# Turning the state's weights on the vector engine in 16 pieces, and a new place for the normalisation, in a fused attention and gated feed-forward kernel

## The chip, the cores and the metric

The kernel runs on one core of a Trainium2 chip. The metric is the device time of one execution in microseconds (us). Runs of a kernel before and of a changed kernel were taken in turn on the same chip.

## The reference, cut to what matters

```python
# x: (8, 8, 512, 64), state: (8, 8, 32, 64)
a      = softmax(scale * x @ state.T);   xread = a @ state     # per batch and head
a2     = softmax(scale * state @ x.T);   sread = a2 @ x
tokens = concat(xread, sread)            # per batch 512 + 32 rows of 512 columns
h      = tokens @ w_in                   # 512 -> 2048
out    = (h * cos(h)) @ w_out            # 2048 -> 512
```

`a` is the side of the tokens, `a2` that of the state. `a2` is computed with the state's rows on the partitions and the 512 tokens along them. For `a2 @ x` it has to stand the other way round, with the tokens on the partitions. This turning is what the change is about.

## The kernel before

Each batch of 512 tokens is worked through in 16 steps, one tile of 128 hidden columns each. The batch's own attention is prepared in the steps of the batch before it, in the gaps. A step's work, by engine:

- PE: `hidden` (L469 in the profile of before), the two products that make a tile of h; then `output`, the products of the tile of three steps ago with w_out (L534).
- ACT and DVE in turn, the gates: `gate` (ACT, L475), `gate2` (DVE, L478), `gate3` (ACT Abs and Sin, L483 and L484), `gate4` (DVE, L490). `gate4` frees the PSUM tile of h, of which there are two, so `hidden` of step s+2 waits for `gate4` of step s.
- In the gaps: PE makes `products` 0 to 3 (the four quarters of state @ w_in, from which `hidden` is made) and `reads` 0 and 1 (the two halves of `a2 @ x`). ACT does `exps`, the exponentials of both softmaxes. DVE does `spread1`, which lays maxima and sums out along the rows, and `norm1`.

The outputs use sums and differences of blocks (seven products for eight). Batches go in pairs, and the accumulators are two pairs of PSUM banks, MAIN and SIDE. At the end of phases 0 and 2, that is in step 10 of each batch, MAIN is copied out, one half by ACT and one by DVE:

```python
def keep_product(out, bank):
    nc.scalar.activation(out.t[:, 0], acc[bank][0], func=ACTF.Copy, scale=TWO_PI)
    nc.vector.tensor_scalar(out.t[:, 1], acc[bank][1], TWO_PI, None, op0=ALU.mult)
```

The turning and what follows it (note that `a2T` takes the place of `spread`):

```python
self.spread, self.z2 = xT[:, 0:2], xT[:, 2:4]          # z2: exp on the state's side
self.a2T = xT[:, 0:2].rearrange("p j (c m) -> p j c m", c=NC)
def turn(self, j):                       # PE, 4 transposes of 128x128 into PSUM
    for c in range(NC):
        nc.tensor.transpose(out=at[j][:, P * c:P * c + P],
                            in_=self.z2[:, j, P * c:P * c + P], identity=ident)
def turn_kept(self, j):                  # ACT, copy from PSUM
    nc.scalar.copy(self.a2T[:, j].rearrange("p c m -> p (c m)"), at[j])
def norm1(self):                         # DVE, a = exp * (1 / sum)
    nc.vector.tensor_tensor(self.aT, self.z1, self.spread, op=ALU.mult)
```

A plan says in which step each part is issued. The lists `x_dve` and `x_act` are issued between `gate2` and `gate3` of the step, `y_act` and `y_dve` behind `gate4`. `later` holds delayed adds and stores, of which one is issued per step ("the pop"). Each engine works in the order of issue.

```python
gate(t); gate2(t); go(1); go(3)          # go(1): x_act, go(3): x_dve
...
gate3(t)
if later: later.pop(0)()
gate4(t)
...
go(2); go(4)                             # y_act, y_dve
...
output(line.pop(0))                      # step 10: ends with keep_product
```

## Time and profile before

| | before |
|---|---|
| median of the first 3 runs | 792.2 us (791.26 to 793.64) |
| median of the 6 runs beside the changed kernel | 791.51 us (791.21 to 793.64) |
| span of the profiled execution | 789.4 us |
| PE busy | 767.3 us (97%) |
| DVE / ACT busy | 431.2 / 389.3 us |

PE's busy share bounds the time.

### The profile page before, as it was taken

The numbers are of one execution on the slowest core, as the hardware profiler recorded it, in microseconds if no ns is written. First come the engines' busy times: TensorE is split into PE (matmuls) and PEld (weight loads), VectorE is DVE, ScalarE is ACT, GpSimd is POOL, SyncE is SP. The second block draws the span as 40 slices with busy tenths as digits, with TensorE's granted clock in tenths as the row PEclk, the third lists the DMA queues.
The fourth block names the chain that finished last, engine by engine and source line by source line (L and its number), as shares of the span: only waits on it lengthen the run. The fifth ranks groups of instructions, "written<-read, shape, count | busy, mean of one in ns | idle before, by whom it ended". The sixth has DMA issues, their size and how long they took to land.

```text
span 789.4 us, 7555 instructions
## 1 busy us (share of the span) xinstructions
PE 767.3 (97%) x2664; PEld 340.4 (43%) x2664; DVE 431.2 (55%) x675; ACT 389.3 (49%) x626; POOL 178.7 (23%) x119
## 2 busy tenths in 40 slices
PE   8998999899999999999999999999999999999997
PEld 3442333344344344444444434434444444455554
DVE  5879887732564467744554467635553545431531
ACT  3877964644364445643473446443563445322222
POOL 3343359684000000551000000740000004610200
PEclk9999999999999999999999999999999999999999
DMA  8485461051010610150003410340100114000021
GB/s 239 160 248 179 127 140 28 0 90 18 0 27 14 107 27 14 30 104 0 15 14 54 80 27 7 53 75 0 27 1 0 27 27 117 17 0 15 14 41 40
DMA packets 161957, 43.49 MB, mean 55 GB/s; under 512 B 153920, under 2 KB 153920, under 8 KB 161920
## 3 DMA queue, kind: packets, MB, share of 16 engines
q1 hardware_dynamic: 161024, 42.49, 24.7%
q10 hardware_dynamic: 768, 0.39, 0.2%
q8 instruction: 21, 0.34, 0.2%
q0 software_dynamic: 128, 0.13, 0.1%
q14 instruction: 16, 0.13, 0.1%
HBM read 34.08 MB, written 8.91 MB: 54 GB/s over the span
## 4 chain that ended last, share of the span: by engine, by line
PE 80%; ACT 9%; DVE 8%; issue 1%; DMA 1%; POOL 1%; SPq 0%; DVEq 0%; POOLq 0%
PE o L534 44%; PE h L469 26%; PE at L316 4%; PE o L654 3%; PE at L406 2%; DVE q L478 1%; ACT q L483 1%; ACT q L484 1%; DVE g_all L490 1%; ACT s L227 1%; ACT q L475 1%; DVE xT L336 1%; ACT xT L362 1%; DVE aT L383 1%; PE o L316 1%
## 5 line engine op out<-in xcount | busy, mean ns | idle before, releaser
L469 PE MATMUL h<-aT,sw 128*128 128x512 f32 x512 | 243.2, 598 | 10.8 <-DVE g_all L490 10.2
L534 PE MATMUL o<-g_all,w_out 128*128 128x512 f32 x512 | 236.4, 598 | 1.1 <-POOL w_out L241 1.1
L496 POOL TENSOR_TENSOR g_all<-g_all 128x512 f32<-128x512 f32 x80 | 112.1, 1424 | 450.8 <-DVE g_all L490 447.2
L475 ACT ACTIVATE q<-h 128x512 f32<-128x512 f32 (+1 forms) x144 | 82.2, 571 | 261.7 <-PE h L469 261.6
L478 DVE SCALAR_TENSOR_TENSOR q<-q,h 128x512 f32<-128x512 f32 (+1 forms) x144 | 94.2, 654 | 207.3 <-ACT q L475 207.3
L534 PE MATMUL o<-g_all,s 128*128 128x512 f32 x384 | 177.3, 598 | 0.0
L490 DVE TENSOR_TENSOR g_all<-h,q 128x512 f32<-128x512 f32 (+1 forms) x144 | 94.8, 658 | 123.9 <-ACT q L484 117.7
L469 PEld LDWEIGHTS h<-aT,sw 128*128 128x128 f32 x512 | 96.8, 191 | 136.2 <-issue 110.2
L534 PEld LDWEIGHTS o<-g_all,w_out 128*128 128x128 f32 x512 | 94.0, 190 | 125.5 <-issue 118.4
L483 ACT ACTIVATE q<-q 128x512 f32<-128x512 f32 (+1 forms) x144 | 87.6, 608 | 96.3 <-DVE q L478 96.3
L534 PEld LDWEIGHTS o<-g_all,s 128*128 128x128 f32 x384 | 70.9, 190 | 91.7 <-issue 87.3
L484 ACT ACTIVATE q<-q,halfpi 128x512 f32<-128x512 f32 (+1 forms) x144 | 100.5, 698 | 4.5
L241 POOL TENSOR_TENSOR w_out<-w_out,s 128x1024 int32<-128x1024 int32 x10 | 23.9, 2389 | 79.4 <-DVE w_out L236 79.4
L496 DVE TENSOR_TENSOR g_all<-g_all 128x512 f32<-128x512 f32 x48 | 33.2, 692 | 1.6
L443 ACT COPY sw<-at 128x512 f32<-128x512 f32 x50 | 26.8, 589 | 9.0 <-PE at L316 9.0
L469 PE MATMUL h<-sT,w_in 128*128 128x256 f32 x128 | 30.2, 379 | 0.0
L654 PE MATMUL o<-w_out,g_all 128*128 128x512 f32 x64 | 29.6, 592 | 0.0
L469 PEld LDWEIGHTS h<-sT,w_in 128*128 128x128 f32 x128 | 24.3, 190 | 10.1 <-issue 6.2
L316 PE MATMUL at<-w_in,stT 64*32 64x512 f32 x400 | 27.2, 601 | 0.0
L241 POOL TENSOR_TENSOR w_in<-w_in,s 128x1024 int32<-128x1024 int32 (+1 forms) x10 | 19.7, 1966 | 32.1 <-DVE w_in L236 18.6
L540 DVE SCALAR_TENSOR_TENSOR held<-o,held 128x512 f32<-128x512 f32 x40 | 25.3, 676 | 2.3 <-PE o L534 2.3
L561 DVE STREAM_TRANSPOSE ot<-held 128x512 f32<-128x512 f32 x32 | 22.2, 692 | 0.0
(83 smaller groups left out, 443.5 us busy)
## 6 DMA issues: line engine op xcount, KB each, us to landing
out_dram<-ot SPq DMA_DIRECT2D x132, 64.0 KB, 2.0
g_all<-in_moe_w_out_dram SPq DMA_DIRECT2D x8, 1024.0 KB, 4.9
g_all<-in_moe_w_in_dram SPq DMA_DIRECT2D x6, 1024.0 KB, 5.2
xT<-in_x_dram SPq DMA_DIRECT2D x96, 64.0 KB, 2.3
x_b<-in_x_dram SPq DMA_DIRECT2D x24, 256.0 KB, 4.7
x_b<-in_x_dram SPq DMA_DIRECT2D x16, 128.0 KB, 3.9
g_all<-in_moe_w_in_dram SPq DMA_DIRECT2D x4, 512.0 KB, 6.0
x_b<-in_moe_w_out_dram SPq DMA_DIRECT2D x1, 1024.0 KB, 6.1
```

The costliest lines, as they stand in the source:

```text
L241: nc.gpsimd.tensor_tensor(bits, bits, e.bitcast(I32), op=ALU.add)
L316: nc.tensor.matmul(out=(to or at)[j][Ns * k:Ns * k + Ns, 0:n], lhsT=w[D * j:D * j + D, self.b, Ns * k:Ns * k + Ns], rhs=r(slice(D * j, D * ...
L443: (copy or nc.scalar.copy)(sw_of[self.b, nt][:, j, c0:c1], to[j][:, 0:c1 - c0])
L469: nc.tensor.matmul(out=t.hp, lhsT=t.lhs(i), rhs=t.rhs(i), start=(i == 0), stop=(i == t.kn - 1))
L475: nc.scalar.activation(t.q, t.hp, func=ACTF.Copy, bias=MAGIC)
L478: nc.vector.scalar_tensor_tensor(out=t.q, in0=t.q, scalar=MAGIC, in1=t.hp, op0=ALU.subtract, op1=ALU.subtract)
L483: nc.scalar.activation(t.q, t.q, func=ACTF.Abs)
L484: nc.scalar.activation(t.q, t.q, func=ACTF.Sin, bias=halfpi, scale=-TWO_PI)
L490: nc.vector.tensor_tensor(t.g, t.hp, t.q, op=ALU.mult)
L496: engine.tensor_tensor(out, a, b, op=ALU.subtract)
L534: nc.tensor.matmul(out=acc[bank][ch], lhsT=w[:, i, P * ch:P * ch + P], rhs=g.g, start=(i == 0), stop=(i == NH - 1))
L654: nc.tensor.matmul(out=acc[MAIN][i], lhsT=t.g[:, P * i:P * i + P], rhs=w_out[:, :, t.f, :], start=(t.n_th == 0), stop=(t.n_th == NF - 1))
```

## The change

The intent: PE no longer turns `a2` for batches 2 to 7. DVE does it, in 16 pieces of 32 partitions. `norm1` of these batches moves behind `gate4`, so that the gate need not wait for it. The pop moves behind `gate4` in steps where `x_dve` has work. Other parts shift by some steps to make room.

```diff
+        def turn_block(self, k, q):
+            src = self.z2.rearrange("p j (c q i) -> p q (j c) i", q=P // 32, i=32)
+            dst = self.a2T.rearrange("p j c m -> p (j c) m")
+            rows = slice(Ns * k, Ns * k + Ns)
+            nc.vector.transpose(out=dst[32 * q:32 * q + 32, :, rows],
+                                in_=src[rows, q])
 ...
-            x_dve[s[6]].append((b, "norm1"))
+            (x_dve if b == 1 else y_dve)[s[6]].append((b, "norm1"))
 ...
-            pairs(s[0], b, "turn", "turn_kept", 0)
+            if b < 2:
+                pairs(s[0], b, "turn", "turn_kept", 0)
 ...
+        def blocks_turned(b, to):
+            for i in range(16):
+                to[i * 5 // 16].append((b, "turn_block", i % NK, i // NK))
 ...
-                prod(14, b + 1, 0)
-                early(b + 1, (1 + (b == 1), 2 + (b == 1), 5, 6, 7, 8, 9))
-                late(b + 1, (10, 11, 12, 15))
+            if b + 1 < B and odd:
+                prod(13, b + 1, 0)
+                early(b + 1, (2, 3, 5, 6, 7, 8, 9))
+                blocks_turned(b + 1, (x_dve[12], y_dve[12], x_dve[13],
+                                      y_dve[13], x_dve[14]))
+                pe[15].append((b + 1, "reads", 0))      # reads 1: next step 0
+            elif b + 1 < B:
+                early(b + 1, (4, 5, 6, 7, 8, 9, 10))
+                blocks_turned(b + 1, (y_dve[10], x_dve[11], y_dve[11],
+                                      x_dve[12], y_dve[12]))
+                late(b + 1, (None, 13, 14))
+                prod(15, b + 1, 0)
 ...
-        if later:
+        if later and not todo[3]:                       # todo[3]: x_dve
             later.pop(0)()
         gate4(t)
 ...
+        if later and todo[3]:
+            later.pop(0)()
         go(4)
```

Left out: batch 1's products 3 are copied by ACT instead of DVE, five conversions of weights come a step later, six of the GpSimd blocks come one step later and two ten, the turning of the tokens comes one or three steps later, other products move by one or two, and in step 3 the copy of batch 0's products 1 moves behind `gate3`.

More of the change, by code (lines that the diff above doesn't have):

```diff
@@ L395, in turn_kept @@
                            at[j])
+        def turn_block(self, k, q):
+            src = self.z2.rearrange("p j (c q i) -> p q (j c) i", q=P // 32,
+                                    i=32)
+            dst = self.a2T.rearrange("p j c m -> p (j c) m")
+            rows = slice(Ns * k, Ns * k + Ns)
+            nc.vector.transpose(out=dst[32 * q:32 * q + 32, :, rows],
+                                in_=src[rows, q])
         def reads(self, j):
@@ L752, in prod @@
             pe[s].append((b, "products", nt) + bank)
-            if b == 1 and nt > 0:
+            if b == 1 and 0 < nt < 3:
                 x_dve[s].append((b, "products_taken", nt) + bank)
@@ L768, in early @@
                 for k in range(NK):
-                    to = (x_dve, y_dve)[k % 2]
+                    to = (x_dve, y_dve)[k % 2 * (k < 2)]
                     to[s[k // 2]].append((b, "tokens_turned", k))
@@ L778, in early @@
             y_dve[s[5]].append((b, "spread1"))
-            x_dve[s[6]].append((b, "norm1"))
+            (x_dve if b == 1 else y_dve)[s[6]].append((b, "norm1"))
         def late(b, s):
-            pairs(s[0], b, "turn", "turn_kept", 0)
-            pe[s[1]].append((b, "reads", 0))
+            if b < 2:
+                pairs(s[0], b, "turn", "turn_kept", 0)
+            if s[1] is not None:
+                pe[s[1]].append((b, "reads", 0))
             pe[s[2]].append((b, "reads", 1))
@@ L804, in plan @@
         else:
+            odd = b % 2
             bank = (SIDE,) if b == 1 else ()
@@ L807, in plan @@
                 turned(1, 0)
-            prod(0, b, 1, *[MAIN for _ in bank])
-            prod(4, b, 2, *bank)
-            prod(9, b, 3, *bank)
-            if b + 1 < B:
-                prod(14, b + 1, 0)
-                early(b + 1, (1 + (b == 1), 2 + (b == 1), 5, 6, 7, 8, 9))
-                late(b + 1, (10, 11, 12, 15))
+                prod(0, b, 1, MAIN)
+            elif odd:
+                prod(0, b, 1)
+                turned(b, 1)
+            else:
+                late(b, (None, None, 0))
+                prod(2, b, 1)
+                turned(b, 3)
+            prod(4, b, 2, *bank)
+            prod(9 if odd else 10, b, 3, *bank)
+            if b + 1 < B and odd:
[10 more added lines that the diff above has]
+                prod(15, b + 1, 0)
         return pe, x_act, y_act, x_dve, y_dve
     conv_at = {s: 4 + i for i, s in enumerate(
-        (0, 1, 2, 3, 4, 5, 6, 7, 8, 10, 11, 12, 13, 14))}
+        (0, 1, 2, 3, 4, 5, 6, 7, 8, 11, 12, 13, 14, 15))}
     conv_at.update({B * NF + 5: N_LOADS, B * NF + 7: N_LOADS + 1})
@@ L825 @@
     lo, hi = slice(0, NH // 2), slice(NH // 2, NH)
-    block_at = {15: (ALU.add, s1, a21, a22, lo),
-                17: (ALU.add, s1, a21, a22, hi),
-                18: (ALU.subtract, s2, s1, a11, lo),
-                19: (ALU.subtract, s2, s1, a11, hi),
-                20: (ALU.subtract, s4, a12, s2, lo),
-                21: (ALU.subtract, s4, a12, s2, hi),
-                22: (ALU.subtract, s3, a11, a21, lo),
-                23: (ALU.subtract, s3, a11, a21, hi)}
+    block_at = {16: (ALU.add, s1, a21, a22, lo),
+                18: (ALU.add, s1, a21, a22, hi),
+                19: (ALU.subtract, s2, s1, a11, lo),
+                20: (ALU.subtract, s2, s1, a11, hi),
+                21: (ALU.subtract, s4, a12, s2, lo),
+                22: (ALU.subtract, s4, a12, s2, hi),
+                32: (ALU.subtract, s3, a11, a21, lo),
+                33: (ALU.subtract, s3, a11, a21, hi)}
     LAG = 3
@@ L871 @@
                 part(0, "products", 1, SIDE)
-                part(0, "products_kept", 1, SIDE)
             go(1)
@@ L881 @@
         gate3(t)
-        if later:
+        if step == 3:
+            part(0, "products_kept", 1, SIDE)
+        if later and not todo[3]:
             later.pop(0)()
```

## The prediction

> **What bounds the kernel now.** I read the page's busy row, then the waits sorted by length, then PE alone in 10 us stretches, and last the timeline of one odd and one even batch.
>
> ```profile
> PE 767.3 (97%) x2664; PEld 340.4 (43%) x2664; DVE 431.2 (55%) x675; ACT 389.3 (49%) x626; POOL 178.7 (23%) x119
> PE 80%; ACT 9%; DVE 8%; issue 1%; DMA 1%; POOL 1%; SPq 0%; DVEq 0%; POOLq 0%
> ...
> PE h L469 <- DVE g_all L490: 10.2, 9, 2.7
> ```
>
> The first line is the share of busy time, the second the chain that ended last, the third the only PE wait of any size: `hidden` waits for `gate4` (L490) to give back one of its two PSUM tiles. PE has work in 767.3 of 789.4 us. Of the 22 idle us, 3.2 lie in the first 10 us and 5.0 in the last 10, where nothing changes. From 160 to 780 us the stretches show PE at 10.00 of 10 us, except 320:330 and 490:500 (9.29 each), in the middle of batches 3 and 5. So nearly any PE time taken away comes off the end, and any wait put before PE is added to it. DVE, at 55%, has room on average, but it works in program order, and the gates of each tile stand in that same queue.
>
> **What the turning costs PE.** Batch 4, in order of time (start, duration, engine, line):
>
> ```profile
> 409.36 1.21 DVE L383 TENSOR_TENSOR aT<-aT,xT 128x1024 f32<-128x1024 f32 x1
> ...
> 409.62 1.88 PE L469 MATMUL h<-aT,sw 128*128 128x512 f32 x4
> ...
> 411.33 1.04 PE L389 MATMUL at<-ident,xT 128*128 128x128 f32 x8
> ...
> 412.20 3.60 PE L534 MATMUL o<-g_all,w_out 128*128 128x512 f32 x8
> ```
>
> From 411.33 to 412.20 the eight transposes hold PE for 0.87 us. There is no penalty around them: `hidden` before takes 409.62 to 411.33 = 1.71 us, and the next starts at 415.64, after 3.44 us for eight matmuls, both the ordinary pace (429 ns each).
>
> **What the Trainium skill says.**
> - "VectorE: DVE Perf Modes", section "The three transpose paths": the vector engine transposes only 32x32 blocks, TensorE a full 128x128 into PSUM. Hence 16 pieces, which together move the blocks; and the copy from PSUM (L394) goes. The trace agrees in that L394 exists only for PE's way: 16 copies of 576 ns.
> - "TensorE: Matmul & The Clock Gate", section "Part 4: PE-mode transpose": about 275 ns in a kernel. L389's mean is 273 ns, but that is latency; eight take 0.87 us, 109 ns each, and that is what is saved.
> - "VectorE: DVE Perf Modes", section "Two Vector instructions with no wait between them": an instruction starts only when all before it are done, if its start quadrant differs from theirs. The pieces change their input quadrant each time. `keep` does so today, and the trace agrees: four of 285 ns take 1.18 us, a step of 298 ns, while two same-quadrant subtractions (L353) of 680 ns take 1.28 us, a step of 600.
> - "Advanced Engine Details and Errata", section "The Read-Write Bubble": a fixed latency per instruction, so small pieces pay it each. The next lines agree.
>
> ```profile
> L561 DVE STREAM_TRANSPOSE ot<-held 128x512 f32<-128x512 f32 x32 | 22.2, 692 | 0.0
> L336 DVE STREAM_TRANSPOSE xT<-i 128x1024 f32<-128x1024 f32 x16 | 19.8, 1236 | 0.0
> ...
> L416 DVE TENSOR_TENSOR sr<-at,i 32x128 f32<-32x128 f32 x32 | 9.1, 285 | 0.3
> ```
>
> 512 elements take 692 ns and 1024 take 1236: 1.06 ns each and about 150 fixed. A piece has 32 partitions by 8 blocks by 32 = 256 elements: estimate 420 ns, with a step of about 435.
>
> **The change, part by part.**
> 1. *Removed:* 6 batches x 8 transposes, 6 x 0.87 = 5.2 us of PE, on the path; 12 copies x 576 ns = 6.9 us of ACT, beside PE.
> 2. *Added:* 96 pieces x 435 ns = 42 us of DVE (431 becomes about 473), 7.0 us per batch. Between gate2 and gate4 DVE waits some 1.45 us for ACT's Abs and Sin (timeline of a step: gate2 ends 3.2 us after the start of `hidden`, gate4 starts at 4.75). Three pieces (1.3 us) fit; four (1.74) push gate4 by 0.3.
> 3. *Moved:* `norm1` from between gate2 and gate4 to behind gate4; the pop of the delayed adds and stores behind gate4 where the slot is taken; reads, products, conversions and four GpSimd blocks by one to ten steps, their number unchanged. Each `products` or `reads` costs PE 1.02 us plus two switches of 0.1 wherever it stands.
>
> *Odd batches 3 and 5 (turning for 4 and 6).* The exps, with a table load before and after them, make the gates of steps 8 to 10 late:
>
> ```profile
> 323.43 0.65 DVE L478 SCALAR_TENSOR_TENSOR q<-q,h 128x512 f32<-128x512 f32 x1
> ...
> 324.00 1.80 DVE L383 TENSOR_TENSOR aT<-aT,xT 128x1024 f32<-128x1024 f32 x1
> ...
> 325.73 0.70 DVE L561 STREAM_TRANSPOSE ot<-held 128x512 f32<-128x512 f32 x1
> ...
> 326.36 0.65 DVE L490 TENSOR_TENSOR g_all<-h,q 128x512 f32<-128x512 f32 x1
> ...
> 327.06 1.98 PE L469 MATMUL h<-aT,sw 128*128 128x512 f32 x4 [0.71 <-DVE g_all L490]
> ```
>
> Without the turn PE wants the last of these at 325.3. Now `norm1` no longer stands before gate4(9), but step 8's store transpose moves behind gate4(8), where nothing hides it: gate2(9) comes at 324.1, the second store transpose follows, Abs and Sin end at 326.15, gate4(9) at 326.95. PE waits 1.65 us instead of 0.71. `hidden` of step 12 then starts at 332.15; before, at 333.53, with 1.2 us of reads that now stand elsewhere. Gain 0.2 us a batch. The pieces, in steps 12 to 14, lie beside steps of 5.16 us or more with reads in step 15: no wait.
>
> *Batch 1.* Nothing is delayed there, and the copy of products 3 (1.28) and `norm1` (2.11) both leave the slot of step 9. gate4(9) ends at about 154.25 instead of 155.93; PE, without its turn, wants it at 154.1. `hidden` of step 12 moves from 162.46 (161.26 without the reads) to 159.5: gain 1.75 us, of which 0.87 is the turn.
>
> *Even batches 2, 4, 6 (turning for 3, 5, 7).* Today they have no PE idle. I count from `hidden` of step 8, which now holds the exps. By the trace's same stretch around its own exps (394.67: the late gate4 starts at 407.02) gate4(9) starts at 12.35. Then: spread1 to 14.15; gate2(10); gate4(10) 16.3 to 17.0; norm1 1.2; four pieces 1.74; keep_product 0.69, so gate2(11) only at 20.5; three pieces, gate4(11) to 23.35; three pieces; gate2(12) at 24.65; three pieces; gate4(12) to 27.5; the last three to 28.8. PE reaches reads(0) of step 13 at 3.44 + 5.16 + 6.36 + 5.16 + 5.16 + 1.72 = 27.0. So reads(0) waits about 1.9 us, where 0.87 was saved: a loss of 1.0 us a batch. With pieces of 0.33 us there would be hardly a wait.
>
> *Batch 0.* A conversion leaves step 10 and one is added at step 15; the long waits there (2.67 us at 80.09, 1.78 at 107.28) come from steps 9 and 14, which keep theirs. I put 0.
>
> *Sum:* -1.75 - 2 x 0.2 + 3 x 1.0 = +0.9 us as reckoned. The wait for the pieces is the shakiest term: their duration is extrapolated, and the slots look as if sized so that they just fit. I take 1.0 us for it in place of 1.9, so +0.1 a batch, and get -1.75 - 0.4 + 0.3 = -1.9 us: 790.3 us.
>
> **The rivals.**
> - *All PE time comes off and no wait appears.* For it: PE at 10.00 of 10 us in the even batches, DVE at 4 to 7 of 10. Then 5.2 + 0.9 = 6.1 us: 786. Against it: the DVE queue as added up for steps 9 to 12.
> - *DVE's queue becomes the bound after the exps.* Gate2 of steps 11 and 12 stands behind 7 us of pieces. If a piece takes 0.5 us or more, or is further delayed by the gates, the even batches lose 2 us or more each and the odd ones have gate4(12) late: 795 to 797.
> - *The reload of tokens comes late.* reads(1) now stands in step 0 or 14, and the tokens are turned four steps later instead of five. Against it: in batch 4 sixteen loads are issued within some 14 us and land 2.3 us after (page), and four steps last 20 us or more. If it fails, each batch waits 1 to 2 us, 6 to 10 us in all.
> - *GpSimd's block differences (s3) in steps 32 and 33 come late for step 35.* Two blocks of 2.4 us, POOL idle there: no effect.
>
> **Range and chances.** The three ways reach from 786 to 797; runs of the kernel before spread over 2.4 us. Range 785.5 to 795.0. Two per cent is 15.8 us, three times all that the turn costs PE. Faster by over 2% would need the start-up stretch to shrink by 10 us; slower by over 2% would need two rivals together. Chances: 0.02, 0.96, 0.02.
>
> **What would show it.** L389 with 16 instructions and about 2.1 us instead of 8.3; L394 four copies; a new DVE group of 96 transposes of about 420 ns; DVE busy about 473 us, PE about 762. PE waiting for DVE at `reads` (L406) in three even batches, 0.5 to 2 us each; `hidden` waiting up to 1.7 us in steps 10 and 11 of batches 3 and 5; less of it in batch 1. I am wrong if the pieces differ much from 420 ns, if reads never wait (then 786 or so), or if tokens_turned waits for a DMA.

## The result, and the profile after

The changed kernel took 799.05 us (median of 6 runs, 796.7 to 799.91) against 791.51 us. The ratio was 1.0087, with a 95% interval of 1.0069 to 1.0105. The change made the kernel slower by 0.9%. The time lies outside the range of the prediction, 785.5 to 795.0.

How the lines read: a wait line has the waiting engine, tile and line, what it waited for, the total in us, the number of waits and the longest. A line of a group ends with the number of instructions, busy us, the mean of one in ns, and idle us before them. A line of a timeline has start and duration in us, engine, line, operation, output and inputs, and the number of instructions; a bracket gives the idle time before and what ended it.

First the page's busy row and chain, then PE's waits (total us, times, longest us), then the groups of pieces and of PE's remaining transposes, all of the changed kernel. Line numbers have moved: `hidden` is L479, `output` L544, `gate4` L500, `keep_product` L555 (ACT) and L557 (DVE), the reads L416, the pieces L404.

```profile
PE 767.4 (96%) x2616; PEld 336.4 (42%) x2616; DVE 471.1 (59%) x769; ACT 384.5 (48%) x616; POOL 181.3 (23%) x119
...
PE 69%; DVE 14%; ACT 12%; issue 2%; DMA 1%; POOL 1%; SPq 0%; DVEq 0%; POOLq 0%
```

```profile
PE h L479 <- DVE g_all L500: 11.4, 9, 2.7
PE o L544 <- DVE held L557: 4.3, 5, 1.2
PE o L544 <- ACT held L555: 3.5, 2, 1.7
...
PE at L416 <- DVE xT L404: 0.6, 3, 0.2
```

```profile
L404 DVE STREAM_TRANSPOSE xT<-xT 32x256 f32<-32x256 f32 x96 | 41.8, 436 | 1.9
...
L389 PE MATMUL at<-ident,xT 128*128 128x128 f32 x16 | 2.1, 276 | 0.0
```

The chain that ended last has 69% PE instead of 80%, and DVE and ACT together 26% instead of 17%. The pieces cost what was expected, 436 ns each, and PE has 48 transposes fewer (2616 matmuls instead of 2664). Its busy time did not fall all the same: `hidden` was busy 1.2 us longer in all (244.4 for 243.2), `output` 2.6 (416.3 for 413.7) and the reads 1.3 (18.8 for 17.5). Four matmuls of `hidden` behind a wait show 1.98 us for 1.88, and 3.52 where they ran at half clock (at 105.36; the clock is treated below). What is new are 7.8 us of waits that did not exist before: `output` waits for `keep_product`, 4.3 us for DVE's half and 3.5 us for ACT's.

To see where the time went I compare stretches in which both kernels do the same work: from the start of products 2 of one batch (step 4) to that of the next, read from PE's timeline in the profiled executions.

| stretch, us | before | after |
|---|---|---|
| start to batch 1 | 125.97 | 125.58 |
| batch 1 to 2 | 83.27 | 81.83 |
| batch 2 to 3, 4 to 5, 6 to 7 | 85.05 each | 86.2 each |
| batch 3 to 4 | 86.02 | 90.23 |
| batch 5 to 6 | 86.02 | 88.54 |

Each even batch loses 1.2 us (3 x 1.2 = 3.5), batches 3 and 5 lose 4.2 and 2.5, the first two rows win 1.8. The sum is 8.4 us, which is the difference of the spans (797.7 - 789.4 = 8.3) within the reading.

**An odd batch, before.** The timeline of the kernel before in batch 3, behind the lines that the prediction shows: gate2 and Sin of step 10, ACT's and DVE's half of `keep_product`, and PE's products of step 11.

```profile
327.64 0.68 DVE L478 SCALAR_TENSOR_TENSOR q<-q,h 128x512 f32<-128x512 f32 x1
...
329.02 0.72 ACT L484 ACTIVATE q<-q,halfpi 128x512 f32<-128x512 f32 x1
...
329.99 3.70 PE L534 MATMUL o<-g_all,s 128*128 128x512 f32 x8
330.12 0.60 ACT L545 ACTIVATE held<-o 128x512 f32<-128x512 f32 x1
...
331.11 0.69 DVE L547 TENSOR_SCALAR held<-o 128x512 f32<-128x512 f32 x1
```

Of the eight matmuls the first four go to SIDE and the last four to MAIN. They reach MAIN at 329.99 + 4 x 0.43 = 331.7. ACT had left its half at 330.7, and DVE leaves the other at 331.8, which the last two want at 332.6. Nothing waits, because PE had spent time on the turn and on reads(0) just before.

**An odd batch, after.** The same place in batch 5, which has no half-clock spell (see below):

```profile
502.66 1.98 PE L479 MATMUL h<-aT,sw 128*128 128x512 f32 x4 [1.39 <-DVE g_all L500]
...
503.25 2.29 DVE L383 TENSOR_TENSOR aT<-aT,xT 128x1024 f32<-128x1024 f32 x1
504.48 1.88 PE L544 MATMUL o<-g_all,s 128*128 128x512 f32 x4
505.46 0.67 DVE L488 SCALAR_TENSOR_TENSOR q<-q,h 128x512 f32<-128x512 f32 x1
...
506.83 0.72 ACT L494 ACTIVATE q<-q,halfpi 128x512 f32<-128x512 f32 x1
507.46 0.58 ACT L555 ACTIVATE held<-o 128x512 f32<-128x512 f32 x1
...
508.09 1.13 PE L544 MATMUL o<-g_all,s 128*128 128x512 f32 x2 [1.73 <-ACT held L555]
...
508.92 0.68 DVE L557 TENSOR_SCALAR held<-o 128x512 f32<-128x512 f32 x1
...
509.65 1.13 PE L544 MATMUL o<-g_all,s 128*128 128x512 f32 x2 [0.44 <-DVE held L557]
```

Read it backwards. PE's matmuls into MAIN wait until 508.09 for ACT's copy. That copy is ready to run as soon as PE has ended step 10, but in ACT's queue it stands behind Abs and Sin of step 10. These wait for gate2 of step 10 (505.46), and gate2 stands behind `norm1`, which takes 2.29 us here and 1.22 in the even batches. GpSimd is at work beside it here and idle there. From the times it looks as if one of the two waits for the other: in batch 1 `norm1` took 1.21 us beside GpSimd (at 153.77), and there two GpSimd instructions took 3.53 us, for 2.51 in the same place before. No run takes GpSimd away, so this is not shown. Then DVE's copy stands behind gate4 in the same way, and PE waits again. With the longer wait for `hidden` (1.39 us instead of 0.71) the batch has 3.56 us of waits in place of 0.71.

**An even batch, after.** Batch 2, where there was no wait at all before:

```profile
243.02 0.58 ACT L555 ACTIVATE held<-o 128x512 f32<-128x512 f32 x1
...
243.82 1.22 DVE L383 TENSOR_TENSOR aT<-aT,xT 128x1024 f32<-128x1024 f32 x1
245.07 1.77 DVE L404 STREAM_TRANSPOSE xT<-xT 32x256 f32<-32x256 f32 x4
246.78 0.64 DVE L557 TENSOR_SCALAR held<-o 128x512 f32<-128x512 f32 x1
...
247.48 1.13 PE L544 MATMUL o<-g_all,w_out 128*128 128x512 f32 x2 [1.15 <-DVE held L557]
...
254.60 1.38 DVE L404 STREAM_TRANSPOSE xT<-xT 32x256 f32<-32x256 f32 x3
255.40 0.43 PE L416 MATMUL at<-x_b,xT 128*64 128x128 f32 x2
...
256.03 1.09 PE L416 MATMUL at<-x_b,xT 128*64 128x128 f32 x14 [0.20 <-DVE xT L404]
```

`norm1` and four pieces stand before DVE's half of `keep_product`, and PE waits 1.15 us for it. Later PE starts reads(0) and must stop for the last pieces. The two waits (1.35 us) and the slow restarts behind them, some 0.7 us, are more than the 0.87 us saved.

**The clock.** The ten microseconds from 330 in the changed kernel (columns: PE, PEld, DVE, ACT and POOL busy, then the granted clock, DMA share, GB/s):

```profile
330.00:340.00 10.00, 7.92 (x14) 3.27 (x15) 5.53 (x10) 4.83 (x9) 6.21 (x5) 0.83 0.00 0
```

The single microseconds from 334 to 337 show 0.50, half the clock. A mean of 0.83 over 10 us is then 3.4 us at half clock: 1.7 us of PE's work lost. Such a spell followed the waits of batch 3 but not the same waits of batch 5, which explains 4.2 us there against 2.5. (In the third run below no spell fell into these two batches, and their stretches took 87.96 and 87.94 us.) The profiled execution of before has one spell in the working stretch, at 80 us; that of the changed kernel has two, at 105 and 334.

### The profile page after: what moved, and what is told of

It is laid out like the page before. It is cut to its first block, busy times and chain, and to the rows that moved or that the text cites. A ratio compares the mean times of both kernels' runs of the same rounds, so it can differ in the third digit from the quotient of the medians.

```text
span 797.7 us, 7549 instructions
## 1 busy us (share of the span) xinstructions
PE 767.4 (96%) x2616; PEld 336.4 (42%) x2616; DVE 471.1 (59%) x769; ACT 384.5 (48%) x616; POOL 181.3 (23%) x119
## 4 chain that ended last, share of the span: by engine, by line
PE 69%; DVE 14%; ACT 12%; issue 2%; DMA 1%; POOL 1%; SPq 0%; DVEq 0%; POOLq 0%
PE o L544 37%; PE h L479 22%; PE o L664 3%; PE at L316 3%; DVE q L488 3%; ACT q L493 3%; ACT q L494 3%; DVE g_all L500 2%; DVE xT L404 2%; PE at L416 2%; ACT xT L362 1%; ACT q L485 1%; DVE xT L336 1%; ACT L494 1%; ACT aT L357 1%
## 5 line engine op out<-in xcount | busy, mean ns | idle before, releaser
L479 PE MATMUL h<-aT,sw 128*128 128x512 f32 x512 | 244.4, 600 | 12.4 <-DVE g_all L500 11.4
L544 PE MATMUL o<-g_all,w_out 128*128 128x512 f32 x512 | 237.2, 599 | 4.6 <-DVE held L557 3.5
L506 POOL TENSOR_TENSOR g_all<-g_all 128x512 f32<-128x512 f32 x80 | 114.8, 1456 | 453.4 <-DVE g_all L500 453.3
L544 PE MATMUL o<-g_all,s 128*128 128x512 f32 x384 | 179.1, 600 | 4.4 <-ACT held L555 3.5
L500 DVE TENSOR_TENSOR g_all<-h,q 128x512 f32<-128x512 f32 (+1 forms) x144 | 95.2, 661 | 112.7 <-ACT q L494 109.1
L479 PEld LDWEIGHTS h<-aT,sw 128*128 128x128 f32 x512 | 97.3, 192 | 138.7 <-issue 113.6
L544 PEld LDWEIGHTS o<-g_all,w_out 128*128 128x128 f32 x512 | 93.8, 190 | 130.7 <-issue 120.7
L544 PEld LDWEIGHTS o<-g_all,s 128*128 128x128 f32 x384 | 70.9, 190 | 100.1 <-issue 87.2
L404 DVE STREAM_TRANSPOSE xT<-xT 32x256 f32<-32x256 f32 x96 | 41.8, 436 | 1.9
L479 PE MATMUL h<-sT,w_in 128*128 128x256 f32 x128 | 30.2, 379 | 0.0
L479 PEld LDWEIGHTS h<-sT,w_in 128*128 128x128 f32 x128 | 24.3, 190 | 10.1 <-issue 6.2
```

What stands on the lines that cost most here:

```text
L404: nc.vector.transpose(out=dst[32 * q:32 * q + 32, :, rows], in_=src[rows, q])
L479: nc.tensor.matmul(out=t.hp, lhsT=t.lhs(i), rhs=t.rhs(i), start=(i == 0), stop=(i == t.kn - 1))
L500: nc.vector.tensor_tensor(t.g, t.hp, t.q, op=ALU.mult)
L506: engine.tensor_tensor(out, a, b, op=ALU.subtract)
L544: nc.tensor.matmul(out=acc[bank][ch], lhsT=w[:, i, P * ch:P * ch + P], rhs=g.g, start=(i == 0), stop=(i == NH - 1))
```

## The experiments

Theory A, formed from these traces: the pieces are not dear. Time is lost because work was put before `gate2` and `keep_product` in DVE's queue, and PE waits for the bank MAIN; and in the even batches because reads(0) comes too early for the last pieces. Rival B: the pieces load DVE and slow everything. Rival C: the moved products and reads cost PE the time. All kernels were compared with the kernel before on the same chip. "Even" and "odd" in the results are the stretches of the table above, from batch 2 to 3 and from 5 to 6 (before 85.05 and 86.02, changed kernel 86.22 and 88.54).

### The pieces left out

```diff
-                to[i * 5 // 16].append((b, "turn_block", i % NK, i // NK))
+                pass
```

> The changed kernel without its 96 pieces; the reads take stale weights, so the state rows are wrong on purpose. Theory A (the loss of the even batches is the pieces standing before keep_product and before reads in the vector engine's queue, the loss of the odd batches is norm1 and the popped store standing before gate2 of step 10): even batches lose their waits of 1.15 + 0.2 us and the slow restarts, some 2.0 us each, odd batches stay as they are: 799 - 6 = 793 us, still slower than before (791.5), with the wait of 1.7 us on ACT's keep_product still there in batches 3 and 5. Rival B (the pieces load DVE and slow all): faster than before, 786 or so, and no wait on keep_product left. Rival C (PE's loss comes from the moved products and reads alone): 799, unchanged.

Measured: 793.23 us, ratio 1.0018 (1.0003 to 1.0033), state rows wrong as intended. Even 84.18, odd 88.54. PE's waits:

```profile
PE o L544 <- ACT held L555: 3.5, 2, 1.7
...
PE o L544 <- DVE held L557: 0.9, 2, 0.4
```

The even batches gain exactly what the turn costs (85.05 - 84.18 = 0.87), the odd ones are as slow as with the pieces. So the pieces cost 2.0 us in each even batch, through the waits, and nothing in the odd ones. Even with the pieces free, the changed kernel is not faster than before. Rival B falls, and C for the even batches; for the odd ones the next run and the one with `keep_product` earlier decide.

### norm1 back before gate4

```diff
-            (x_dve if b == 1 else y_dve)[s[6]].append((b, "norm1"))
+            x_dve[s[6]].append((b, "norm1"))
```

> Only norm1 put back before gate4 for all batches. Theory A: in batches 3 and 5 the wait for gate4 grows from 1.40 to about 2.5 us, but the wait on ACT's keep_product (1.73) disappears and that on DVE's stays near 0.4, so 0.5 to 1.5 us gained in each odd batch; in batch 1 some 0.8 us lost; even batches the same or slightly worse: 797 to 799 us. Rival B (pieces): no change, 799. If norm1's place were the whole cause: 791 to 793.

Measured: 791.66 us, ratio 1.0001 (0.9986 to 1.0016). Even 84.94, odd 86.93, batch 1 82.03 (81.83 with the change). PE's waits:

```profile
PE o L544 <- DVE held L557: 0.9, 2, 0.4
...
PE at L416 <- DVE xT L404: 0.6, 3, 0.2
```

My expectation was a miss by 5 us. In the odd batches it held: 1.6 us gained each, no wait on ACT's half. But I had left out that `norm1` stands before `keep_product` in the even batches as well. Taken from there it goes into the time in which DVE waits for ACT anyway, the wait of 1.15 us disappears, and each even batch gains 1.3 us. With 3 x 1.3 + 2 x 1.6 = 7.1 us, putting `norm1` back takes away nearly the whole loss. In the even batches it is not the only cause: without the pieces the loss is gone there as well. `norm1` and the pieces are one queue in front of PE, and what the two runs gain must not be added.

### The pop back before gate4

```diff
-        if later and not todo[3]:
+        if later:
             later.pop(0)()
 ...
-        if later and todo[3]:
-            later.pop(0)()
```

> Only the pop of the delayed adds and stores put back before gate4 in every step. Theory A: in batches 3 and 5 gate2 of step 9 comes 0.65 us earlier, the wait for gate4(9) falls from 1.40 to about 0.75 us and the wait on ACT's keep_product is unchanged at 1.7: about 1.3 us gained in all, 797.5 us. Rival B: no change. If the pop were the whole cause: 793 or less.

Measured: 796.06 us, ratio 1.006 (1.0043 to 1.0076). Even 86.21, odd 87.94. In batches 3 and 5 the wait for `gate4` fell from 1.40 to 0.81 us and that on ACT's half stayed at 1.72. The pop's new place costs 0.6 us in each odd batch and nothing in the even ones. The median fell by more than twice 0.6; the profiled execution had one spell at half clock, the changed kernel's two, and I don't assign the rest.

### Both back

The two diffs above together.

> norm1 and the pop both back. Theory A: the odd batches are about what they were before the change less the turn, some 2 us faster each than in the changed kernel, plus a half-clock spell fewer (1.7 us): 793.5 to 796 us; the even batches keep their 1.15 + 0.2 us of waits. Rival B: no change, 799.

Measured: 790.4 us, ratio 0.9985 (0.9969 to 1.0002). Even 84.95, odd 86.52. It came out better than expected because of the even batches, as in the second run. No wait for ACT's half was left. The turn is gone from PE, and yet nearly nothing is gained: the next runs ask where it went.

### PE's turn taken out of the kernel before, nothing put in

```diff
-            pairs(s[0], b, "turn", "turn_kept", 0)
+            if b < 2:
+                pairs(s[0], b, "turn", "turn_kept", 0)
```

> The kernel before with nothing but PE's 48 transposes and their copies taken out (no pieces, nothing moved; state rows wrong on purpose). If every transpose were on the path: 791.5 - 5.2 = 786.3 us. If, as the trace of before suggests, in batches 1, 3 and 5 the PE only waits longer for gate4(9) (0.98 to 1.85 us, and 0.71 to 1.58 twice), the gain is only that of the three even batches: 3 x 0.87 = 2.6 us, 789 us.

Measured: 789.81 us, ratio 0.9973 (0.9956 to 0.9989), state rows wrong as intended. Even 84.17, odd 86.02, batch 1 83.27. PE's waits for `gate4` in this kernel:

```profile
PE h L469 <- DVE g_all L490: 12.9, 9, 2.7
```

Before it was 10.2 us in as many waits. The difference of 2.7 us is 3 x 0.87: in batches 1, 3 and 5 PE waits for `gate4` of step 9 as much longer as it works less. So of the 5.2 us of transposes only those of the three even batches, 2.6 us, were on the path. (In the start-up a PE wait of 1.7 us for a copy by ACT is new, where the kernel before had its spell at half clock and this execution has none; the stretch to batch 1 took 126.11 us for 125.97.)

### reads(0) of the even batches beside reads(1)

On top of "both back":

```diff
-                late(b + 1, (None, 13, 14))
+                late(b + 1, (None, 14, 14))
```

> norm1 and pop back as in the fourth run, and in the even batches reads(0) moved from step 13 to 14, beside reads(1), which takes away its wait for the last pieces without touching the pieces. If that wait is where the even batches' gain of 0.87 us went: an even batch falls from 84.95 to about 84.0 us, no PE wait on pieces left, 790.4 - 3 x 0.95 = 787.5 us. If the pieces cost something else (a slower DVE or PE beside them): 84.9 again and 790.

Measured: 788.53 us, ratio 0.996 (0.9943 to 0.9976), correct. Even 83.99, odd 86.52. No PE wait on L404 is left. The even batches' gain had gone into the wait for the last pieces, and it comes back with a step more, with the pieces where they were. The total is 1 us above the expectation; the profiled execution had three spells at half clock in the working stretch, at 79, 106 and 151 us.

### keep_product earlier, norm1 where the change put it

```diff
+            if s == 10 and t.b in (1, 3, 5):
+                while len(line) >= LAG:
+                    output(line.pop(0))
             go(1)
             go(3)
 ...
+        if s == 10 and t.b in (2, 4, 6):
+            while len(line) >= LAG:
+                output(line.pop(0))
         go(4)
```

> The changed kernel with norm1 where the change put it, and only keep_product emitted earlier: in the odd batches behind gate2 of step 10, in the even ones before norm1 and the pieces. If the bank held by keep_product is the way by which norm1's new place costs time: odd batches lose their waits of 1.73 and 0.44 us and fall from 88.5 to about 86.1 us; even batches lose the wait of 1.15 us but then wait as much longer at reads(0) for the last pieces (0.2 becomes about 1.8), so stay near 86.2. In all 2 x 2.4 us and a half-clock spell: 792.5 to 794.5 us. If the bank isn't the way: 799.

Measured: 794.74 us, ratio 1.0034 (1.0019 to 1.0049), correct. Even 86.24, odd 86.35. PE's waits:

```profile
PE h L479 <- DVE g_all L500: 11.5, 10, 2.7
PE at L416 <- DVE xT L404: 4.7, 6, 1.1
```

This shows the way. No wait on `keep_product` is left, in any batch; the odd batches fall by 2.2 us although `norm1` stands where it stood. In the even batches the wait moved to reads(0): 1.57 us in each (4.7 / 3), in place of 1.15 and 0.20. The last piece sets the end there, whichever of PE's two waits it is booked under. The total is just above the expected 794.5 us; the profiled execution had a spell at half clock in batch 4, from 430 to 433, and that stretch took 87.94 us.

### norm1 moved in the kernel before

```diff
-            x_dve[s[6]].append((b, "norm1"))
+            (x_dve if b == 1 else y_dve)[s[6]].append((b, "norm1"))
```

> The kernel before with norm1 of batches 2 to 7 moved behind gate4, nothing else. If norm1's new place is harmful by itself: +7 us as between the changed kernel and the second run, 798 us. If it is harmful only once PE's turn and reads no longer stand between the products of steps 10 and 11 (before, PE reaches the bank at 331.7 in batch 3, after ACT has left it at about 331.6), then no PE wait on keep_product appears, an odd batch gains up to 0.7 us and the whole is 790 to 792 us.

Measured: 791.8 us, ratio 1.0012 (0.9995 to 1.0029), correct. Even 85.05, odd 86.92, batch 1 82.02.

```profile
PE h L469 <- DVE g_all L490: 7.8, 6, 2.7
PE at L406 <- ACT xT L394: 3.2, 2, 1.6
```

Neither side of the expectation was right for the odd batches. The wait for `gate4` is gone there, as the change intended, but PE now waits 1.6 us at reads(0) for ACT's copy of the turned weights. The timeline of batch 3 in this run:

```profile
325.58 2.29 DVE L383 TENSOR_TENSOR aT<-aT,xT 128x1024 f32<-128x1024 f32 x1
...
327.94 0.59 ACT L394 COPY xT<-at 128x512 f32<-128x512 f32 x1 [3.25 <-PE h L469]
...
328.58 1.09 PE L406 MATMUL at<-x_b,xT 128*64 128x128 f32 x16 [1.61 <-ACT xT L394]
```

The copy overwrites the tile (`xT`, the part named `spread`) from which `norm1` reads, and it starts when `norm1` has ended, at 325.58 + 2.29 = 327.87. The page books ACT's wait under PE, whose turn had long been done (it started at 322.31 and takes 1.04 us), so I read it by the times. In all the move loses 0.9 us in an odd batch of the kernel before and nothing in an even one; in batch 1 it gains 1.25. By itself it costs little. In the changed kernel it costs the 7 us of the second run: in the odd batches with the turn and reads(0) gone from between the products of steps 10 and 11, in the even ones with the pieces behind it in the queue.

### Only the pieces, on the kernel before

```diff
-            pairs(s[0], b, "turn", "turn_kept", 0)
+            if b < 2:
+                pairs(s[0], b, "turn", "turn_kept", 0)
 ...
-                prod(14, b + 1, 0)
+                prod(13, b + 1, 0)
 ...
-                late(b + 1, (10, 11, 12, 15))
+                to = (x_dve[11], y_dve[11], x_dve[12], y_dve[12], x_dve[13])
+                for i in range(16):
+                    to[i * 5 // 16].append((b + 1, "turn_block", i % NK, i // NK))
+                late(b + 1, (None, 14, 14, 15))
```

`turn_block` is the one of the change.

> The kernel before with only the pieces in place of PE's turn: pieces in steps 11 to 13, both reads in step 14, products 0 of the next batch in step 13; norm1, pops, conversions, tokens and batch 1's products as before. If the pieces cost nothing where no wait hangs on them: even batches 85.05 - 0.87 - 0.2 = 84.0 us, odd batches 86.0 to 86.5 (their gain is eaten by the wait for gate4(9)), in all 788.5 to 790 us. If the pieces slow DVE or PE in themselves: 791 or more.

Measured: 788.0 us, ratio 0.9956 (0.9941 to 0.997), correct. Even 83.82, odd 86.16. The core of the change alone, with the pieces where almost nothing hangs on them (PE waits 0.23 us on DVE's half in batches 3 and 5), is a small gain. The 42 us of DVE work are nearly free: with the turn simply left out (above) the stretches were 84.17 and 86.02. Against that run the even batch also has both reads in one step.

### A version that beats both

On top of "reads(0) beside reads(1)", for the odd batches:

```diff
-                early(b + 1, (2, 3, 5, 6, 7, 8, 9))
+                early(b + 1, (2, 3, 5, 6, 7, 8, 10))    # norm1 in step 10
 ...
+            if s == 10 and t.b in (1, 3, 5):            # keep_product behind gate2
+                while len(line) >= LAG:
+                    output(line.pop(0))
             go(1)
             go(3)
 ...
-        if later:
+        if later and not (t.b in (3, 5) and s in (8, 9, 10)):
             later.pop(0)()
```

> The fifth run, and in the odd batches 1, 3 and 5 norm1 in step 10 between gate2 and gate4, the outputs of step 10 (with both halves of keep_product) right behind gate2, and no pops in steps 8 to 10 of batches 3 and 5. If the odd batches' loss is made of the wait for gate4(9) (1.4 to 1.6 us) and for keep_product alone, both nearly vanish: an odd batch falls from 86.5 to about 85.0 us and the whole to 783.5 to 785.5 us, about 1% faster than before the change. If something else holds them: 787.

Measured: 786.1 us, ratio 0.9924 (0.9905 to 0.9944), correct. Odd 85.25. The even stretch from batch 2 is 84.34, with one wait of 0.25 us on DVE's half; the other two are 83.99 and 83.98. The total is 0.6 us above the expected range. PE's waits for `gate4`, and the one left on `keep_product`:

```profile
PE h L479 <- DVE g_all L500: 9.8, 8, 2.7
...
PE o L544 <- DVE held L557: 0.3, 1, 0.3
```

The wait for `gate4` in batches 3 and 5 is 0.81 us each, where "both back" had 1.58. Three things were moved at once for the odd batches; no run says what each of them gave. The same kernel again, with more rounds:

> The sixth run's kernel again, with more rounds for a narrower interval: 784.5 to 787 us, ratio 0.991 to 0.994.

Measured: 785.68 us (4 runs, 783.74 to 785.71), ratio 0.992 (0.9906 to 0.9935). By the ratio it is 0.8% faster than the kernel before; by the medians, taken on different chips, it is 1.7% faster than the changed one (785.68 / 799.05).

## Why the prediction was wrong

It gave 790.3 us, 1.9 us less than before; measured were 7.5 us more. Its chance of 0.96 for less than 2% either way held (0.9% slower), its range did not. Point by point, by its own steps:

- **The bound and the pieces: right.** The cost of a piece (estimate 420 ns with a step of 435; 436 ns measured, four in 1.77 us) and DVE's sum (estimate 473 us; 471.1) held, and in the odd batches the pieces cost nothing, as it says. PE's busy time did not: some 762 us were expected and 767.4 measured, for the reasons given with the profile after.
- **Batch 1: right in size.** Predicted -1.75 us; the stretch shortened by 1.44, and the start-up, put at 0, by 0.4, which no run separates. Its split, 0.87 of it for the turn, is not borne out: the turn alone taken out left this stretch at 83.27, and `norm1` alone moved brought it to 82.02.
- **Odd batches, the step that failed.** The step reads: "`hidden` of step 12 then starts at 332.15 ... Gain 0.2 us a batch." Up to `hidden` of step 11 its reckoning fits: from `hidden` of step 10 it has 326.95 - 321.88 = 5.07 us, and the changed kernel's batch 5 shows 502.66 - 497.67 = 4.99. But then it lets the products of step 11 run at once. It saw that `norm1` no longer stands before gate4 of step 9, and did not ask what it stands before now: gate2 of step 10, through it Abs and Sin, and behind these ACT's half of `keep_product`. `keep_product` is missing from this step, and in the even batches it is only work in DVE's queue; who waits for it is never asked. The products into MAIN do, and their waits of 1.73 and 0.44 us with the restarts are the difference of 2.7 us: a loss of 2.5 us a batch in place of a gain of 0.2, and in the profiled execution in batch 3 a spell at half clock (1.7 us of PE's work) behind them. The run with `keep_product` earlier shows this way directly.
- **Even batches: the reckoning was right, and the discount wrong.** The reckoning has a loss of 1.0 us a batch, from a last piece that ends 28.8 us after `hidden` of step 8. Measured: a loss of 1.2 us, with the last piece at 255.98, that is 29.1 us after `hidden` of that step (226.92). I then put 1.0 us for the wait of 1.9, because the slots "look as if sized so that they just fit". A guess about how the schedule came about replaced the sum, and took 2.7 us off the prediction. Here too the wait on `keep_product` was missed, but it did not add: PE arrives later at reads(0) by what it has waited already.
- **The turn.** The prediction counted 5.2 us "on the path". The trace that it read shows waits for `gate4` in batches 1, 3 and 5, and there a shorter PE only waits longer. It found this for batch 3, in its own step, but did not say that half of the 5.2 us could not be gained in any arrangement that leaves those gates as late as they are. The run without the turn shows 2.6 us.
- **The rivals.** "DVE's queue becomes the bound after the exps", at 795 to 797 us, came nearest: that queue sets the end in the even batches, though they lose 1.2 us each and not 2 or more; in the odd batches it was not the pieces but `norm1`. The late reload of tokens and late GpSimd blocks did not occur: no PE wait on them is in the changed kernel's list.

With the measured terms its sum comes out: 792.2 - 0.4 - 1.4 + 2 x 2.5 + 3 x 1.2 = 799.0 us, and 798.3 from the later median of 791.51, without counting the additional half-clock spell of some executions.

Two slips in its readings had no effect: the last 10 us of the kernel before have 4.4 us without PE work and not 5.0 (its stretch ran past the end), and eight GpSimd blocks move, not four.

## What to carry to other kernels

When work is put into an in-order queue, list everything behind it in that queue and who waits for each item: here not only the gate of the tile, but a copy that frees an accumulator bank, which had been hidden by the very work that the change removed. "Out of the way" of one consumer is in the way of the next; in the even batches the idle time of DVE between gate2 and gate4, in which ACT works, was the place that delayed nothing. In the odd ones `norm1` there makes PE wait longer for `gate4` (1.58 us with both back, 0.81 with only the pop back), which was still the smaller loss. And when a sum has been worked out from a trace, don't discount it because the schedule looks deliberate.

## What the Trainium skill lacked or had wrong

- "TensorE: Matmul & The Clock Gate", section "Part 4: PE-mode transpose", gives some 275 ns for one bfloat16 transpose in a kernel, and no pace for several in a row. The float32 transposes here last as long (273 ns), but eight 128x128 in a row took 0.87 us, 109 ns each, and taking them away saved 0.87 us where they were on the path.
- The same page, section "Part 1: The HAM clock gate (the "warmup" mystery)", names an idle window of about 3.4 us as what brings the half clock. Here spells of some 3.4 us at half clock (1.7 us of PE's work each) came with single waits of at most 2.7 us, in the run with `keep_product` earlier behind waits of 1.06 and 0.51 us, and not with the same waits in each batch or each execution. No run settles the condition.
- "VectorE: DVE Perf Modes", section "The three transpose paths", gives one time for the vector engine's transpose, for bfloat16, and no law for float32: 256 elements on 32 partitions took 436 ns, 512 elements on 128 partitions 692, 1024 took 1236. Its rule on held instructions, in "Two Vector instructions with no wait between them", agrees: four pieces took 1.77 us, a step of 445 ns.
- "Advanced Engine Details and Errata", section "GPSIMD Details", says that GpSimd shares an interface with DVE and conflicts with its instructions that have two inputs in SBUF, without a size. `norm1` has two such inputs. It took 1.22 us with GpSimd idle (batch 2) and 2.29 us beside it (batch 5), but in batch 1 only 1.21 us beside it, with GpSimd slower there by 1.0 us. Which of the two waits, no run here settles.
